# RetNet attention and a gated MLP in one kernel: loads of v behind k, scaling of v on Pool, a third value bank, four more steps transposed by TensorE

## The chip, the cores and the metric

The kernel runs on one core of a Trainium2 chip. A time is the device time of one execution, in microseconds. The compute engines are TensorE (PE, with its weight loads as PEld), VectorE (DVE), ScalarE (ACT) and GpSimd (POOL); SyncE (SP) only issues DMAs here. Each engine takes its instructions in order, and engines wait for each other and for DMAs through semaphores.

## The reference

Eight batches, eight heads, 576 positions, 64 columns a head. The retention has no softmax, only a decay by distance; its result goes through two matrix products with a gelu (sigmoid form) between them.

```python
scores = scale * np.matmul(q, k.transpose(0, 1, 3, 2))
gamma = 1.0 - 2.0 ** (-5.0 - np.arange(H))
rel = pos[:, None] - pos[None, :]
Dmat = np.where(rel >= 0, gamma[:, None, None] ** rel[None, :, :], 0.0)
attn_out = np.matmul(scores * Dmat, v)
x = attn_out.transpose(0, 2, 1, 3).reshape(B * S, H * D)     # 4608 x 512
h = x @ w_in                                                  # 512 x 2048
out = (h * (1.0 / (1.0 + np.exp(-1.702 * h)))) @ w_out        # 2048 x 512
```

## The kernel before, in words

A batch is cut into five chunks of 128 positions (the last has 64), so there are 40 steps; step n is batch n // 5, chunk n % 5. The decay is separated: v is multiplied by a growing factor by key position (`scale_v`, L255, one multiplication of 128 x 512 on VectorE), the result by a falling one by query position (`evac_o`, L356). Inside a chunk the scores are masked to the lower triangle (`mask_s`); what earlier chunks contribute goes through a running state Z = sum of k times v, kept in PSUM (`psZ`) and copied to bf16 by ScalarE in two halves (`evac_z`, L348).

A step is: bring q and k in transposed form into a buffer `qk` (four buffers), `scores` (L281), `mask_s`, `values` (L302: scores times v, the state's update, and the earlier state times q), then `evac_o`, which writes the transposed activations `xT`, and `evac_z`. The transposed form comes in one of two ways. `turn` or a `burst` below step `PE_TURNS` has TensorE transpose (`transposes`, L265, eight matmuls with the identity into `psT`) and ScalarE copy the result out (`evac_t`, L277). From step `PE_TURNS` on, `dma_turn` (L365) has SP issue two DMA transposes, three steps ahead.

The second part works on 512 tokens at a time, nine times. `hidden` (L407) does four matmuls and a gelu on ScalarE for each of 16 column groups, through two PSUM banks in turn; `project` (L425) does the second product, VectorE copies the result out and SP issues its store.

The order is written by hand: each call records instructions for the engines' queues, and waits come from the recorded reads and writes. The prologue (L442 to L505) does steps 0 to 3 and needs all four before the first `hidden`. There, `fill` (L455) gives TensorE matmuls on zeros. Then the 16 `hidden` groups of the first 512 tokens carry step 4 (`turn(4)`), the first 16 `project` groups carry steps 5 to 8 and their transposes, and the 16 `hidden` groups of the next 512 tokens (L537) carry `intra(9)` and `burst(10)` to `burst(13)`. After that a regular pattern of `project`, `hidden` and bursts follows (`region`, L548).

All inputs are fp32 in HBM. Pool issues the loads that cast to bf16 (queue q0, software descriptors): q and k of chunks 0 to 3 of batch 0, `load_w_in(0)`, chunk 4 (`load(0, 4)`: q, k and v), the other three pieces of w_in, four pieces of w_out, then batches 1 and 2. SP loads v of chunks 0 to 3 of batch 0 as fp32 (`load_v32`, L188; queue q1), at the very start; `scale_v` reads these and writes bf16. Before `load(0, 4)` VectorE clears the lower half of chunk 4 (`constants_third`).

The result of the values product lies in a PSUM bank until `evac_o` has read it; in the prologue steps 0 to 3 take two banks in turn (`half`: `psO` and `psU`).

Of the kernel before, what the change touches and what calls it, by code (L numbers as in the profile page):

```python
# [7 lines left out]
ALU = mybir.AluOpType  # L8
# [4 lines left out]
H = 8  # L13
# [5 lines left out]
HP = 4  # L19
# [4 lines left out]
NF = FF // 128  # L24
NST = 3
NQK = 4
PE_TURNS = 10
QK_SCALE = 1.0 / math.sqrt(DH)

IN_ORDER = ("PE", "ACT", "DVE", "POOL", "SP")  # L30
# [92 lines left out]
def bass_retnet_parallel__then__act_gelu_quick_kernel(  # L123
# [9 lines left out]
    R = Rec()  # L133
    es = ExitStack()
    with es:
# [21 lines left out]
        v32 = sb("v32", [P, 4, H * DH], FP32)  # L157
# [20 lines left out]
        def load(b, c):  # L178
            sl, rows = b % NST, ROWS[c]
            for nm, src, dst in (("q", q, st_q), ("k", k, st_k), ("v", v, st_v)):  # L180
                if nm == "v" and b == 0 and c < 4:
                    continue
                s = src[b, :, 128 * c : 128 * c + rows, :].rearrange("h p d -> p h d")
                d = dst[0:rows, sl, c, :].rearrange("p (h d) -> p h d", d=DH)
                R.op("POOL", lambda e, d=d, s=s: e.dma_start(d, s),  # L185
                     w=[(nm, sl, c)], dma=(nm, sl, c))

        def load_v32(c):  # L188
            s = v[0, :, 128 * c : 128 * c + 128, :].rearrange("h p d -> p h d")
            d = v32[:, c, :].rearrange("p (h d) -> p h d", d=DH)  # L190
            R.op("SP", lambda e: e.dma_start(d, s), w=[("v32", c)], dma=("v32", c))

        def load_w_in(i):
            s = moe_w_in.rearrange("(a p) n -> p a n", p=128)[:, :, 512 * i : 512 * i + 512]
            R.op("POOL", lambda e: e.dma_start(w_in_sb[:, :, 512 * i : 512 * i + 512], s),
                 w=[("w_in", i)], dma=("w_in", i))
# [43 lines left out]
        def constants_third(a, b):  # L240
            for t, nm in ((st_q, "q"), (st_k, "k"), (st_v, "v")):
                R.op("DVE", lambda e, t=t: e.memset(t[64:128, a:b, 4, :], 0.0),
                     w=[(nm, sl, 4) for sl in range(a, b)])
# [8 lines left out]
                 r=[("lng", 0, 0), ("lng", 0, 1)], w=["tiny"])  # L252


        def scale_v(n):  # L255
            b, c = divmod(n, NC)
            sl = b % NST
            t = st_v[:, sl, c, :].rearrange("p (h d) -> p h d", d=DH)
            f = vfac[:, :, c : c + 1].to_broadcast([P, H, DH])
            first = b == 0 and c < 4  # L260
            i = v32[:, c, :].rearrange("p (h d) -> p h d", d=DH) if first else t
            R.op("DVE", lambda e: e.tensor_tensor(t, i, f, ALU.mult),  # L262
                 r=["vfac"] + ([("v32", c)] if first else []), w=[("v", sl, c)])

        def transposes(n):  # L265
            b, c = divmod(n, NC)
            sl = b % NST

            def fn(e):
                for a, t in ((0, st_q), (1, st_k)):  # L270
                    for hp in range(HP):
                        i = e.matmul(psT[:, a, hp, :], t[:, sl, c, 128 * hp : 128 * hp + 128],  # L272
                                     ident.ap(), is_transpose=True)
                return i
            R.op("PE", fn, r=["ident", ("q", sl, c), ("k", sl, c)], ps=["T"])
# [26 lines left out]
        def values(n, o=None, z_last=False):  # L302
            po, key = o or (psO, "O")
            b, c = divmod(n, NC)
            sl, N = b % NST, ROWS[c]

            def av(e):
                for hp in range(HP):
                    for hh in range(2):
                        h = 2 * hp + hh  # L310
                        i = e.matmul(po[64 * hh : 64 * hh + 64, hp, 0:N],  # L311
                                     st_v[:, sl, c, 64 * h : 64 * h + 64],
                                     sm[n % 2][:, hh, hp, 0:N],
                                     start=(hp == 0), stop=(c == 0), skip_group_check=True)
                return i
            R.op("PE", av, r=[("sm", n % 2), ("v", sl, c)], ps=[key])
            def add_state():
                if c < 4:
                    def state(e):
                        for hp in range(HP):  # L320
                            for hh in range(2):
                                h = 2 * hp + hh
                                hs = slice(64 * h, 64 * h + 64)
                                i = e.matmul(psZ[64 * hh : 64 * hh + 64, hp, 0:64],  # L324
                                             st_k[:, sl, c, hs], st_v[:, sl, c, hs],
                                             start=(c == 0 and hp == 0), stop=(c == 3),
                                             skip_group_check=True)
                        return i
                    R.op("PE", state, r=[("k", sl, c), ("v", sl, c)], ps=["Z"])

            def add_inter():
                if c > 0:
                    def inter(e):
                        for hp in range(HP):
                            i = e.matmul(po[:, hp, 0:N], zs[(c - 1) % 2][:, hp, :],  # L335
                                         qk[n % NQK][:, 0, hp, 0:N],
                                         start=False, stop=True, skip_group_check=True)
                        return i
                    R.op("PE", inter, r=[("zs", (c - 1) % 2, 0), ("zs", (c - 1) % 2, 1), ("qk", n % NQK, 0)], ps=[key])

            if z_last:
                add_inter()
                add_state()
            else:
                add_state()
                add_inter()

        def evac_z(n):  # L348
            c = n % NC
            for hh in range(2):  # L350
                rows = slice(64 * hh, 64 * hh + 64)
                R.op("ACT", lambda e, rows=rows: e.activation(  # L352
                    zs[c % 2][rows, :, rows], psZ[rows, :, 0:64], AF.Copy),
                    w=[("zs", c % 2, hh)], ps=["Z"])

        def evac_o(n, o=None):  # L356
            po, key = o or (psO, "O")
            b, c = divmod(n, NC)
            N = ROWS[c]
            t0 = S * b + 128 * c  # L360
            R.op("DVE", lambda e: e.tensor_tensor(  # L361
                xT[:, :, t0 : t0 + N], po[:, :, 0:N], gq[:, c, :, 0:N], ALU.mult),
                r=[("gq", min(c, 1))], w=[("xT", b, c)], ps=[key])
# [9 lines left out]
        def turn(n):  # L373
            transposes(n)
            evac_t(n)
            scale_v(n)

        def intra(n):
            scores(n)
            mask_s(n)  # L380
# [58 lines left out]
                     r=[("osb", m)], dma=("osb", m))  # L439


        for c in range(4):  # L442
            load_v32(c)
        constants_first()
        for c in range(4):
            load(0, c)
        load_w_in(0)
        constants_third(0, 1)
        load(0, 4)
        for i in range(1, 4):  # L450
            load_w_in(i)
        for i in range(4):
            load_w_out(i)
# [1 line left out]
        def fill(count):  # L455
            def fn(e):
                for _ in range(count):
                    i = e.matmul(psH[0].ap(), idle[:, 0:128], idle.ap(), start=True, stop=True)  # L458
                return i
            R.op("PE", fn, r=["idle"], ps=[("H", 0)])  # L460

        half = [(psO, "O"), (psU.ap().rearrange("p (h n) -> p h n", h=HP), "U")]
        fill(16)
        transposes(0)
        later_gq(0)
        evac_t(0)
        scale_v(0)
        constants_second()
        scale_v(1)
        later_gq(1)  # L470
        fill(4)
        intra(0)
        transposes(1)
        evac_t(1)
        scale_v(2)
        fill(3)
        intra(1)
        values(0, half[0])
        evac_z(0)
        transposes(2)  # L480
        evac_t(2)
        evac_o(0, half[0])
        later_gq(2)
        later_gq(3)
        scale_v(3)
        fill(3)
        intra(2)
        transposes(3)
        evac_t(3)
        values(1, half[1])  # L490
        evac_z(1)
        evac_o(1, half[1])
        intra(3)
        values(2, half[0])
        evac_z(2)
        evac_o(2, half[0])
        gelu_table()
        fill(3)
        values(3, half[1], z_last=True)
        evac_o(3, half[1])  # L500
        evac_z(3)
        constants_third(1, NST)
        for b in (1, 2):
# [19 lines left out]

        def values_8():
            values(8)
            dma_turn(12)
            finish(8)
            scale_v(10)

        between = {1: lambda: turn(5), 3: burst_5, 6: lambda: burst(6), 9: lambda: burst(7),  # L530
                   12: lambda: burst(8), 14: values_8}
        for i in range(16):
            r, g = divmod(i, 4)
            project(0, r, g, *wide[r % 3])
            if i in between:
                between[i]()
        between = {0: lambda: intra(9), 3: lambda: burst(10), 6: lambda: burst(11),  # L537
                   9: lambda: burst(12), 12: lambda: burst(13)}
        for f in range(NF):
            hidden(1, f)  # L540
# [91 lines left out]
```

## Time and profile before

| | |
|---|---|
| median of three runs | 316.35 us (316.22 to 316.98) |
| the profiled execution | 318.7 us, its span 316.9 us |
| mean granted clock of TensorE | 0.995 |
| busy in the span: PE, ACT, DVE, POOL | 305.2, 128.1, 121.8, 103.8 us |
| first `hidden` matmul | 22.18 us |
| transposes of step 5, of step 6 | 39.08 and 41.82 us |
| software queue q0, hardware queue q1 | 17.83 MB and 17.97 MB |

The span is from the first to the last instruction; the profiled execution's own time has what lies around it. A time in the profile counts from the span's start. A busy TensorE is a pipelined one, so its share says that it had something in flight. The DMA share can be above 1.00, as packets of one engine overlap.

### The profile page before, as it was taken

To read this page: it belongs to the slowest core of one execution; us is meant where nothing else is said; L and a number is where in the kernel's file an instruction comes from. 1 tells how busy PE (TensorE), PEld (TensorE's weight loads), DVE (VectorE), ACT (ScalarE), POOL (GpSimd) and SP (SyncE) were. 2 spreads that over 40 slices of the span, in tenths; PEclk is the share of its full clock that TensorE was granted. 3 is DMA by queue.
4 is the path that set the end of the run, shared out by engine and by line. 5 is a ranking of instruction groups with operands and counts; after the bars stand their busy time and mean duration, and the time that the engine had idled before them with its cause. 6 is when DMAs were issued, how large, how long until landed. Compare 5 with 4: busy or idle time off the path is not lost.

```text
span 316.9 us, 5362 instructions
## 1 busy us (share of the span) xinstructions
PE 305.2 (96%) x2285; PEld 147.1 (46%) x2285; DVE 121.8 (38%) x180; ACT 128.1 (40%) x237; POOL 103.8 (33%) x131
## 2 busy tenths in 40 slices
PE   7679999997999999999999999999999999999995
PEld 2344455443445444444445444444444444444442
DVE  6482067573334533433335334334343341010011
ACT  6487543563334433333334333333334333333300
POOL 9996399465585858332500000000000000000000
PEclk9999999997999999999999999999999999999999
DMA  9999999999999999999992223303330000001111
GB/s 146 173 198 206 180 166 171 156 165 155 136 168 168 166 170 175 168 173 156 148 133 60 67 68 83 78 33 87 81 91 35 34 35 33 35 33 49 50 66 69
DMA packets 153048, 36.14 MB, mean 114 GB/s; under 512 B 144320, under 2 KB 148416, under 8 KB 153024
## 3 DMA queue, kind: packets, MB, share of 16 engines
q0 software_dynamic: 112576, 17.83, 81.9%
q1 hardware_dynamic: 40448, 17.97, 27.2%
q8 instruction: 18, 0.29, 0.4%
q14 instruction: 6, 0.05, 0.0%
HBM read 36.70 MB, written 9.44 MB: 146 GB/s over the span
## 4 chain that ended last, share of the span: by engine, by line
PE 91%; DMA 5%; ACT 2%; POOL 1%; DVE 0%; issue 0%; SPq 0%; POOLq 0%; ACTq 0%
PE psH L414 38%; PE psU L428 34%; PE psH L428 4%; PE psO L311 4%; PE psS L290 4%; PE psO L335 3%; DMA st_k<-in_k_dram 2%; DMA qk<-st_k 2%; PE psZ L324 1%; PE psT L272 1%; PE psO L428 1%; ACT qk L278 1%; POOL st_q L185 1%; ACT gq L246 0%; POOL st_k L185 0%
## 5 line engine op out<-in xcount | busy, mean ns | idle before, releaser
L419 ACT ACTIVATE gT<-psH 128x512 bf16<-128x512 f32 x144 | 86.0, 597 | 139.0 <-PE psH L414 139.0
L414 PE MATMUL psH<-xT,w_in_sb 128*128 128x512 bf16 x576 | 140.8, 381 | 0.5 <-DVE xT L361 0.5
L428 PE MATMUL psU<-w_out_sb,gT 128*128 128x512 bf16 x496 | 121.8, 379 | 0.0
L299 DVE TENSOR_TENSOR sm<-psS,mask 128x1024 bf16<-128x1024 f32 (+1 forms) x40 | 44.7, 1117 | 107.9 <-PE psS L290 107.9
L414 PEld LDWEIGHTS psH<-xT,w_in_sb 128*128 128x128 bf16 x576 | 54.5, 98 | 66.6 <-ACT gT L419 4.1
L428 PEld LDWEIGHTS psU<-w_out_sb,gT 128*128 128x128 bf16 x496 | 47.5, 98 | 53.6
L185 POOL DMA_DIRECT2D st_k<-in_k_dram x40 | 35.0, 875 | 36.2 <-PE psO L335 17.0
L436 DVE COPY osb<-psU 128x512 f32<-128x512 f32 x31 | 21.4, 691 | 56.1 <-PE psU L428 55.4
L185 POOL DMA_DIRECT2D st_q<-in_q_dram x40 | 35.2, 880 | 8.7 <-issue 8.2
L185 POOL DMA_DIRECT2D st_v<-in_v_dram x36 | 31.4, 871 | 12.4 <-issue 8.3
L352 ACT ACTIVATE zs<-psZ 64x256 bf16<-64x256 f32 x64 | 24.2, 378 | 16.3 <-PE psZ L324 15.4
L262 DVE TENSOR_TENSOR st_v<-st_v,vfac 128x512 bf16<-128x512 bf16 x36 | 24.6, 682 | 8.0 <-DMA st_v<-in_v_dram 8.0
L361 DVE TENSOR_TENSOR xT<-psO,gq 128x512 bf16<-128x512 f32 (+1 forms) x38 | 23.8, 627 | 9.5 <-PE psO L335 8.8
L290 PE MATMUL psS<-qk 64*128 64x128 bf16 (+1 forms) x320 | 15.1, 213 | 4.3 <-ACT qk L278 2.2
L290 PEld LDWEIGHTS psS<-qk 64*128 64x128 bf16 x320 | 8.7, 94 | 21.2 <-issue 19.8
L278 ACT ACTIVATE qk<-psT 128x1024 bf16<-128x1024 bf16 x10 | 10.2, 1021 | 16.0 <-PE psT L272 15.9
L311 PE MATMUL psO<-sm,st_v 128*64 128x128 bf16 (+1 forms) x304 | 15.2, 222 | 0.0
L428 PE MATMUL psH<-w_out_sb,gT 128*128 128x512 bf16 x64 | 14.5, 379 | 0.0
L311 PEld LDWEIGHTS psO<-sm,st_v 128*64 128x64 bf16 x304 | 9.4, 110 | 4.7 <-issue 1.4
L335 PE MATMUL psO<-qk,zs 128*128 128x128 bf16 (+1 forms) x120 | 11.3, 217 | 0.0
L458 PE MATMUL psH<-idle 128*128 128x512 bf16 x29 | 9.8, 490 | 1.2 <-DVE idle L212 1.2
L324 PE MATMUL psZ<-st_v,st_k 128*64 128x64 bf16 x256 | 9.5, 197 | 0.0
(43 smaller groups left out, 74.3 us busy)
## 6 DMA issues: line engine op xcount, KB each, us to landing
out_dram<-osb SPq DMA_DIRECT2D x36, 256.0 KB, 2.3
st_q<-in_q_dram POOLq DMA_DIRECT2D x32, 128.0 KB, 20.2
st_k<-in_k_dram POOLq DMA_DIRECT2D x32, 128.0 KB, 20.3
st_v<-in_v_dram POOLq DMA_DIRECT2D x28, 128.0 KB, 20.2
w_in_sb<-in_moe_w_in_dram POOLq DMA_DIRECT2D x4, 512.0 KB, 11.7
w_out_sb<-in_moe_w_out_dram POOLq DMA_DIRECT2D x4, 512.0 KB, 18.8
v<-in_v_dram SPq DMA_DIRECT2D x4, 256.0 KB, 5.1
st_q<-in_q_dram POOLq DMA_DIRECT2D x8, 64.0 KB, 19.6
```

The costliest lines, as they stand in the source:

```text
L185: R.op("POOL", lambda e, d=d, s=s: e.dma_start(d, s), w=[(nm, sl, c)], dma=(nm, sl, c))
L262: R.op("DVE", lambda e: e.tensor_tensor(t, i, f, ALU.mult), r=["vfac"] + ([("v32", c)] if first else []), w=[("v", sl, c)])
L290: i = e.matmul(psS[:, hh, hp, 0:N], t[rows, 1, hp, :], t[rows, 0, hp, 0:N])
L299: R.op("DVE", lambda e: e.tensor_tensor(o, i, m, ALU.mult), r=["mask"], w=[("sm", n % 2)], ps=["S"])
L311: i = e.matmul(po[64 * hh : 64 * hh + 64, hp, 0:N], st_v[:, sl, c, 64 * h : 64 * h + 64], sm[n % 2][:, hh, hp, 0:N], start=(hp == 0), stop ...
L335: i = e.matmul(po[:, hp, 0:N], zs[(c - 1) % 2][:, hp, :], qk[n % NQK][:, 0, hp, 0:N], start=False, stop=True, skip_group_check=True)
L352: R.op("ACT", lambda e, rows=rows: e.activation(zs[c % 2][rows, :, rows], psZ[rows, :, 0:64], AF.Copy), w=[("zs", c % 2, hh)], ps=["Z"])
L361: R.op("DVE", lambda e: e.tensor_tensor(xT[:, :, t0 : t0 + N], po[:, :, 0:N], gq[:, c, :, 0:N], ALU.mult), r=[("gq", min(c, 1))], w=[("xT" ...
L414: i = e.matmul(psH[t].ap(), w_in_sb[:, a, 128 * f : 128 * f + 128], xT[:, a, 512 * c : 512 * c + 512], start=(a == 0), stop=(a == 3))
L419: R.op("ACT", lambda e: e.activation(gT[c % 2][:, f, :], psH[t].ap(), AF.Gelu_apprx_sigmoid), w=[("gT", c % 2, f)], ps=[("H", t)])
L428: i = e.matmul(bank, gT[c % 2][:, f, 128 * r : 128 * r + 128], w_out_sb[:, f, :], start=(f == 0), stop=(f == NF - 1))
L436: R.op("DVE", lambda e: e.tensor_copy(osb[m].ap(), bank), w=[("osb", m)], ps=[key])
```

## The change

Four things change, with the order around them.

SP's fp32 load of v for chunk c carries a read of k of chunk c, so SP waits for k's landing before it issues the load. In the recorded order `load_v32(c)` now follows `load(0, c)`.

`scale_v` takes an engine; chunks 1 to 3 of batch 0 are scaled by Pool. On Pool's queue the scaling of chunk 1 stands behind `load_w_in(0)`, that of chunk 2 behind `load_w_in(1)`, that of chunk 3 behind `load(0, 4)`; the other w_in, w_out and later loads follow. Chunk 0 stays on VectorE, now behind `mask_s(0)`.

The prologue has a third value bank (`psH[1]`) for step 3; steps 0 and 2 use `psO`, step 1 `psU`. `transposes(2)` goes ahead of `values(0)`, the fills are 14, 4, 3, 2, 2, 2 matmuls instead of 16, 4, 3, 3, 3, `later_gq(2)` and `later_gq(3)` and the gelu's table load move.

`PE_TURNS` goes from 10 to 14: steps 10 to 13 are transposed by TensorE and copied out by ScalarE, and their eight DMA transposes on SP go. `turn(10)` goes behind `intra(9)`; `dma_turn(12)` and `scale_v(10)` leave `values_8`.

```diff
-PE_TURNS = 10
+PE_TURNS = 14
@@ load_v32
-            R.op("SP", lambda e: e.dma_start(d, s), w=[("v32", c)], dma=("v32", c))
+            R.op("SP", lambda e: e.dma_start(d, s), r=[("k", 0, c)], w=[("v32", c)], dma=("v32", c))
@@ scale_v
-        def scale_v(n):
+        def scale_v(n, eng="DVE"):
...
-            R.op("DVE", lambda e: e.tensor_tensor(t, i, f, ALU.mult),
+            R.op(eng, lambda e: e.tensor_tensor(t, i, f, ALU.mult),
@@ loads
-        for c in range(4):
-            load_v32(c)
         constants_first()
         for c in range(4):
             load(0, c)
+            load_v32(c)
         load_w_in(0)
+        scale_v(1, "POOL")
+        load_w_in(1)
+        scale_v(2, "POOL")
         constants_third(0, 1)
         load(0, 4)
-        for i in range(1, 4):
+        scale_v(3, "POOL")
+        for i in range(2, 4):
             load_w_in(i)
@@ prologue
-        half = [(psO, "O"), (psU.ap().rearrange("p (h n) -> p h n", h=HP), "U")]
-        fill(16)
+        third = [(psO, "O"), (quarters(psU), "U"), (quarters(psH[1]), ("H", 1))]
+        fill(14)
         transposes(0)
         later_gq(0)
         evac_t(0)
-        scale_v(0)
         constants_second()
-        scale_v(1)
         later_gq(1)
         fill(4)
         intra(0)
+        scale_v(0)
         transposes(1)
         evac_t(1)
-        scale_v(2)
+        later_gq(2)
         fill(3)
         intra(1)
-        values(0, half[0])
-        evac_z(0)
         transposes(2)
         evac_t(2)
-        evac_o(0, half[0])
-        later_gq(2)
-        later_gq(3)
-        scale_v(3)
-        fill(3)
+        values(0, third[0])
+        evac_z(0)
+        evac_o(0, third[0])
+        fill(2)
         intra(2)
         transposes(3)
         evac_t(3)
-        values(1, half[1])
+        later_gq(3)
+        values(1, third[1])
         evac_z(1)
-        evac_o(1, half[1])
+        evac_o(1, third[1])
+        fill(2)
         intra(3)
-        values(2, half[0])
+        values(2, third[0])
         evac_z(2)
-        evac_o(2, half[0])
         gelu_table()
-        fill(3)
-        values(3, half[1], z_last=True)
-        evac_o(3, half[1])
+        evac_o(2, third[0])
+        fill(2)
+        values(3, third[2], z_last=True)
+        evac_o(3, third[2])
         evac_z(3)
@@ after step 8
         def values_8():
             values(8)
-            dma_turn(12)
             finish(8)
-            scale_v(10)
+
+        def intra_9():
+            intra(9)
+            turn(10)
...
-        between = {0: lambda: intra(9), 3: lambda: burst(10), 6: lambda: burst(11),
+        between = {0: intra_9, 3: lambda: burst(10), 6: lambda: burst(11),
```

More of the change, by code (lines that the diff above doesn't have):

```diff
@@ L460, in fill, with quarters @@
             R.op("PE", fn, r=["idle"], ps=[("H", 0)])
-        half = [(psO, "O"), (psU.ap().rearrange("p (h n) -> p h n", h=HP), "U")]
-        fill(16)
+        def quarters(bank):
+            return bank.ap().rearrange("p (h n) -> p h n", h=HP)
+        third = [(psO, "O"), (quarters(psU), "U"), (quarters(psH[1]), ("H", 1))]
+        fill(14)
         transposes(0)
```

## The prediction

> **What bounds the kernel now.** I read the shares of the chain that ended last, then the same chain up to 90 us in order of time, then the waits, the stretches of 5 us, the landing times of single loads, and the timeline where ScalarE shares a stage with the transposes.
>
> Shares of the chain, over the whole span:
>
> ```profile
> PE 91%; DMA 5%; ACT 2%; POOL 1%; DVE 0%; issue 0%; SPq 0%; POOLq 0%; ACTq 0%
> ```
>
> TensorE sets the end; what isn't TensorE lies in the first 75 us. The chain up to 90 us (start, us, what):
>
> ```profile
> 4.17 7.56 DMA st_k<-in_k_dram
> ...
> 22.18 1.90 PE psH L414 x8
> ...
> 37.51 1.73 PE psU L428 x8
> 39.24 0.45 PE psT L272 x8
> 39.69 1.73 PE psU L428 x8
> 41.41 0.33 PE psS L290 x8
> 41.74 0.08 issue
> 41.82 0.61 PE psT L272 x8
> ...
> 67.46 7.13 DMA qk<-st_k
> 74.59 0.14 issue
> 74.72 0.47 PE psS L290 x8
> 75.19 0.57 PE psO L311 x8
> 75.76 0.21 PE psZ L324 x8
> 75.98 0.54 PE psO L335 x4
> 76.52 3.55 PE psH L414 x12
> 80.07 0.86 PE psU L428 x4
> ```
>
> Two places matter: the transposes of step 5 and step 6 at 39.24 and 41.82, which seem free, and the scores of step 13 at 74.72, which wait for a DMA transpose issued at 67.46. Waits up to 130 us (line, for what: us, times, longest), then the two 5 us stretches around the wait (busy us of PE, PEld, DVE, ACT, POOL, clock, DMA share, GB/s):
>
> ```profile
> PE psS L290 <- DMA qk<-st_k: 2.2, 1, 2.2
> ```
>
> ```profile
> 70.00:75.00 5.00, 2.83 (x20) 1.15 (x18) 1.63 (x3) 2.23 (x5) 3.45 (x5) 0.99 1.92 156
> 75.00:80.00 5.00, 5.00 (x38) 2.65 (x34) 2.51 (x3) 1.95 (x4) 3.01 (x4) 0.67 1.78 157
> ```
>
> TensorE stands still for 2.2 us and then runs at a granted clock of 0.67. The landing of the one load of k that step 5 needs (issued at 17.28), by its tile:
>
> ```profile
> DMA to landing us min/median/max: 21.6/21.6/21.6
> ```
>
> It lands at 38.9; its transposes start at 39.1. k of step 6, issued at 19.89, takes 21.8 and lands at 41.7; its transposes start at 41.8. So the DMA queue, not TensorE, is within 0.2 us of setting the pace at 39 to 42: whatever shortens TensorE's prologue is lost there, and whatever delays the queue of loads shows in full.
>
> **Part 1, the last four DMA transposes become TensorE's (steps 10 to 13).** Between 58.1 and 80.1 TensorE's pieces at full clock are 16 groups of hidden at 0.86 (13.8), scores, values and states of the five bursts 0.22, 0.79, 0.79, 1.12, 1.12: 17.9 of 22.0 us. The rest is the 2.2 us wait, 1.6 of half clock after it (0.47 for 0.33, 0.57 for 0.34, 0.21 for 0.12, 0.54 for 0.33, 3.55 for 2.59), 0.3 in scraps. Removed: 3.8. Added: four times eight transposes at 0.45 (row 39.24): 1.8. The loads of k for steps 11 to 13 must then be in by about 62, 65 and 69; step 13's lands at 45.60 + 21.2 = 66.8 now, beside six DMA transposes which go, so I cost it at nothing; its cover is the empty queue.
>
> ScalarE gets four evacuations of 1.02 more. Beside step 9 and in the burst of 10 no evacuation of Z stands with them; there the copy for step 4, at 24.62, is the pattern: the twelve hidden matmuls behind it took 2.68 (chain, at 24.53) for 2.59, so 0.1 each. In the bursts of 11 and 12 the order is evacuation of T, two of Z, then gelu. Timeline of the burst of 11 now:
>
> ```profile
> 66.19 0.77 ACT L352 ACTIVATE zs<-psZ 64x256 bf16<-64x256 f32 x2 [0.21 <-PE psZ L324]
> 67.15 0.60 ACT L419 ACTIVATE gT<-psH 128x512 bf16<-128x512 f32 x1 [0.20 <-PE psH L414]
> ```
>
> The gelu ends at 67.75 and TensorE needs that bank at 67.88. With 1.02 ahead: 0.1 + 1.02 + 0.77 + 0.60 + 0.05 = 2.5 against two groups of hidden, 1.7: 0.75 late. Twice: 1.5. Bounds of this stall: 0 (the next group's order absorbs it) and 1.7. Part 1: -3.8 + 1.8 + 1.5 = -0.5 (ends -2.0 and 0).
>
> **Part 2, the fp32 loads of v wait for k.** Now four loads of 256 KB have queue q1 to themselves until 4.0 (1,823 packets), then share: in 6 to 8 us, q0 moves 1,104 packets and q1 967, where q0 alone moves 1,226 in one us (10 to 11). In the changed kernel q0 starts at 4.0 alone, with the issue pace of Pool (0.87 a load) about equal to 1,024/1,226 = 0.84 us a load. First k at about 4.0 + 1.7 + 0.9 of landing = 6.7 (8.9 now), second at 8.4 (11.7 now). But all 4,096 packets of v now come beside q0 instead of some half of them: at 480 a us a v load lasts 2.1 us, in which q0 loses 2.1 x (1,226 - 550) = 1,400 packets or 1.2 us: 4.6 for four. Now the same sum shows as 15.1 (landing of the last k, 7.63 + 7.5) less 4.0 + 6.9 + 0.9: 3.3. So 1.3 us later for what follows in q0, before any wait; ends 0 (v beside weights costs less) and 2.
>
> SP's queue holds nothing else in that time (its next issue is at 42.17). Behind the waiting loads stand the scalings. An SP load takes 3.4 to 7.1 us to land (these four), 6.1 beside a full queue (the two outputs at 42 and 48). v of chunk 1: 8.4 + 4.2 = 12.6; of chunk 2, k at about 11.5, + 4.5 = 16; of chunk 3, k at about 14.5, + 4.5 = 19, with ends 3.4 and 7.1.
>
> **Part 3, three scalings on Pool, in front of its DMA issues.** Behind the first stand w_in 1; behind the second load(0, 4); behind the third w_in 2 and 3, w_out and all loads of batches 1 and 2. No row shows Pool at elementwise work on 512 columns: DVE takes 0.68 for it; Pool's iota makes 128 columns in 0.23, 0.92 for 512 with no input to read. Lower end 0.7, upper 1.8, taken 1.2, by the iota, the nearest row. [...]
>
> Pool then: 8 loads and w_in 0 issued by 9.3 as now; scaling 1 at 12.6 to 13.8; w_in 1 to 14.7; scaling 2 at 16.0 to 17.2; load(0, 4), three at 0.70, to 19.3; scaling 3 to 20.5; w_in 2 issued by 21.4. From the end of an issue to the first packet is 1.6 (q0's first: 2.43 to 4.0), so w_in 2 starts to move at 23.0, 2.5 to move (0.5 MB at 206 GB/s), 0.9 to land: 26.4. Now it lands at 12.02 + 12.3 = 24.3. Everything behind it is 2.1 us late: k of step 5 at 41.0, of step 6 at 43.8. Ends: 0.2 (v of chunk 2 in at 14.4, Pool at 0.8) and 5 (v of chunks 2 and 3 with 7.1 beside the weights).
>
> **Part 4, three banks, fewer fills, order of the prologue.** values(3) is bound by scaling 3: 20.6, where it starts at 20.66 now; so the first hidden group stays near 22.2 (ends 19.5 and 25), and transposes of step 5 could start at 39.1. Two idle matmuls fewer (27 for 29, 0.22 to 0.43 each), within waits. Worth nothing either way, since the queue sets 41.0: TensorE waits 1.9 us there, then 0.1 at step 6: 43.8 for 41.8. A drop of the clock as at 75 would add up to 1.6; taken as 0.
>
> **Sum.** Queue +2.0, part 1 -0.5: +1.5. The profiled execution took 318.7 (span 316.9, 1.8 around it) and would take 320.2; it stands 2.3 over the median of 316.35, and the change goes on the median: 317.8.
>
> **The rivals.**
>
> *The queue isn't starved: faster.* If v of chunk 2 lands by about 14.5 and Pool scales in 0.8, w_in 2 moves on time and the queue is at most 0.5 late. For it: k is in 2 to 3 us earlier than now, Pool needs only one packet ahead of the queue, w_in 0 and 1 are 5 us of work. Against it: 4.5 us to land is already less than the 6.1 seen beside a full queue. It decides where w_in 2 lands: before about 25, the gain of part 1 is larger. Then +0.3 - 0.5 to -2.0: 314.7 to 316.1, middle 315.2.
>
> *The loads of v are starved beside the weights.* While w_in moves, 408 packets go in 2 us; if queues alternate packet by packet, a v load of 1,024 packets needs as many of the weights', 5 us, not 2. v of chunks 2 and 3 then land at about 19 and 21, scaling 3 ends at 24, w_in 2 lands near 29.3: +5.0 - 0.5 = 320.9. [...]
>
> *The two cancel.* The queue about 0.5 to 1.5 late: within 0.3% of now, about 316.4.
>
> **Chances and range.** Differences of 0.3% (0.95 us) or less can't be told from none. Forecast 0.42 (317.3 to 319.2), starved v 0.16, cancelling 0.17, faster 0.25. That gives slower 0.58, same 0.17, faster 0.25. The range leaves a tenth at each end: 314.6 to 321.0; the forecast's own is 317.3 to 319.2.
>
> **What would show it.** In the changed kernel: w_in 2 lands after 25.5; a wait of TensorE at the transposes of step 5, released by the DMA of st_k, at 40 to 42; Pool idle before its scalings, released by the landing of v; no wait at the scores of step 13, clock 1.00 in 75 to 80; waits of 0.7 at hidden groups in the bursts of 11 and 12, released by gelu. It is wrong if step 5's transposes start before 39.5, or if the bursts show no wait behind ScalarE.

## The result, and the profile after

The kernel after takes 324.65 us (median of four runs, 323.68 to 326.89), the kernel before beside it 316.44 us (316.22 to 316.98): a ratio of 1.027, with a 95% interval of 1.021 to 1.032. That is slower, as forecast, but by 8.2 us and not by 1.5, and above the upper end of the range (321.0). Executions of the kernel before vary: of 29 on one chip, 20 took 316.5 to 317.4 us (granted clock 0.998 or more) and the nine with a lower granted clock (0.989 to 0.995) 317.5 to 321.9, of which the ratio there leaves out the longest. The profiled execution of after took 324.11 us, its span is 322.3 us.

Shares of the chain that ended last, in the kernel after:

```profile
PE 84%; DMA 9%; POOL 4%; issue 1%; ACT 0%; DVE 0%; POOLq 0%
```

TensorE falls from 91% to 84%; DMA and Pool rise from 6% to 13%. In order of time (start, us, what), with the pieces left out marked:

```profile
...
5.92 5.11 DMA st_k<-in_k_dram
11.04 7.28 DMA v<-in_v_dram
18.39 1.05 POOL st_v L262
...
21.51 1.08 POOL st_v L262
22.59 1.49 POOL w_in_sb L195 x2
24.08 2.97 POOL w_out_sb L200 x4
27.05 0.82 POOL st_q L185
27.87 16.75 DMA st_k<-in_k_dram
44.75 0.61 PE psT L272 x8
...
47.54 0.61 PE psT L272 x8
...
75.16 0.59 ACT gT L419
...
80.14 0.59 ACT gT L419
```

After Pool's first issues the chain goes through k of chunk 2 to the load of v that waits for it, to the scaling on Pool that waits for that, to the load of k for step 5, which Pool now issues at 27.87 (17.28 before) and which lands at 44.61 (38.92 before). The transposes of step 5 stand at 44.75 (39.24 before), those of step 6 at 47.54 (41.82): 5.5 and 5.7 us later, and nothing of it is won back.

Three of the waits up to 130 us, those on which the reading rests (line, for what: us in all, times, longest):

```profile
POOL st_v L262 <- DMA v<-in_v_dram: 7.2, 2, 6.9
PE psT L272 <- DMA st_k<-in_k_dram: 2.0, 1, 2.0
PE psH L414 <- ACT gT L419: 1.3, 2, 0.7
```

The 2.0 us are only the last part of the delay at step 5. TensorE was ready for these transposes at 42.75, itself 3.5 us later than before, since its prologue is late too: it waits 1.1, 1.4 and 0.4 us for scaled v, its clock is 0.50 from 14 to 26 us, and the first `hidden` starts at 24.70 for 22.18. The late v thus reaches step 5 by two ways, the load queue and the prologue, and the queue is the later one.

Pool's own timeline around the scalings (start, us, what, in brackets the idle time before and its releaser):

```profile
8.52 0.83 POOL L195 DMA_DIRECT2D w_in_sb<-in_moe_w_in_dram  x1
16.23 1.06 POOL L262 TENSOR_TENSOR st_v<-v,vfac 128x512 bf16<-128x512 f32 x1 [6.89 <-DMA v<-in_v_dram]
17.24 0.81 POOL L195 DMA_DIRECT2D w_in_sb<-in_moe_w_in_dram  x1
18.39 1.05 POOL L262 TENSOR_TENSOR st_v<-v,vfac 128x512 bf16<-128x512 f32 x1 [0.35 <-DMA v<-in_v_dram]
...
21.50 1.09 POOL L262 TENSOR_TENSOR st_v<-v,vfac 128x512 bf16<-128x512 f32 x1
22.50 1.58 POOL L195 DMA_DIRECT2D w_in_sb<-in_moe_w_in_dram  x2
```

Pool waits for 6.9 us, and from 9.35 to 17.24 it issues no load. What that does to the transfers is in the 5 us stretches of before (busy us of PE, PEld, DVE, ACT, POOL, then clock, DMA share, GB/s):

```profile
0.00:5.00 5.00, 3.81 (x9) 1.34 (x10) 3.55 (x19) 3.97 (x12) 4.32 (x11) 1.00 0.75 123
5.00:10.00 5.00, 3.53 (x19) 1.57 (x18) 1.98 (x5) 1.46 (x4) 5.00 (x8) 1.00 1.87 184
10.00:15.00 5.00, 3.42 (x55) 2.11 (x53) 2.71 (x3) 2.63 (x4) 5.00 (x9) 1.00 2.32 163
15.00:20.00 5.00, 3.62 (x70) 2.50 (x68) 4.14 (x6) 4.52 (x9) 5.00 (x8) 1.00 1.54 192
20.00:25.00 5.00, 4.46 (x44) 2.33 (x42) 3.96 (x7) 4.26 (x9) 5.00 (x7) 1.00 1.24 207
```

and of after, with two single us in which the software queue moved only 12 and 32 packets:

```profile
0.00:5.00 5.00, 3.81 (x9) 1.34 (x10) 3.54 (x19) 3.96 (x12) 4.31 (x11) 1.00 0.53 34
5.00:10.00 5.00, 4.68 (x37) 2.23 (x35) 1.62 (x4) 3.03 (x6) 4.35 (x6) 1.00 2.07 151
10.00:15.00 5.00, 3.04 (x44) 1.72 (x44) 2.79 (x4) 3.11 (x5) 0.00 (x0) 0.82 1.64 199
15.00:20.00 5.00, 3.64 (x40) 2.34 (x38) 1.92 (x2) 2.39 (x4) 3.42 (x4) 0.50 0.96 164
20.00:25.00 5.00, 3.92 (x46) 2.46 (x44) 2.81 (x4) 2.92 (x6) 5.00 (x8) 0.50 1.29 131
...
18.00:19.00 1.00, 1.00 (x14) 0.62 (x10) 0.16 (x1) 0.75 (x2) 0.65 (x2) 0.50 0.52 37
24.00:25.00 1.00, 0.57 (x9) 0.26 (x8) 0.84 (x2) 0.68 (x2) 1.00 (x3) 0.50 0.73 33
...
75.00:80.00 5.00, 4.30 (x48) 2.33 (x48) 2.42 (x3) 3.36 (x7) 3.88 (x5) 1.00 2.24 158
```

The last column accounts for most of the delay of the loads. Both kernels load the same inputs. Added up (5 us times GB/s), before has moved 1,535 KB by 10 us and 4,345 KB by 25; after has moved 925 and 3,395. The missing 950 KB are 4.6 us at the 206 GB/s at which the weights go (25 to 30 us in before), of the 5.7 us by which k of step 5 is late. 610 KB of it, 3.0 us, are missing already at 10 us: before moves v in the first microseconds, when the software queue has nothing to move yet, and after leaves that time empty (34 GB/s for 123). In 10 to 15, 180 KB are made up. The other 520 KB, 2.5 us, go in 15 to 25, where Pool's late issues let the queue run dry.

The last row answers the stretch that the prediction showed at a clock of 0.67: in after it runs at 1.00. The burst of step 13 itself now stands at 80 to 85 us; the clock is 1.00 there too, and no scores of step 13 wait.

The whole difference sits ahead of 86 us. Here it is cut into three, with a second profile of the kernel before (below), whose time is the ordinary one: the start of the second 512 tokens' first `hidden`, the length of that stretch of 16 groups with its bursts, and the rest of the span.

| us | starts | lasts | rest of the span | span |
|---|---|---|---|---|
| before, profile shown first | 58.08 | 21.99 | 236.8 | 316.9 |
| before, second profile | 58.02 | 19.89 | 236.8 | 314.7 |
| after | 63.80 | 21.73 | 236.8 | 322.3 |

Against the second profile: +5.8 ahead of the stretch (parts 2 to 4), +1.8 in it (part 1), nothing behind it; 7.6 together, which is the difference of the spans.

### The profile page after: what moved, and what is told of

Its sections match the earlier page's. It is cut to its first block, busy times and chain, and to the rows that moved or that the text cites. A ratio compares the mean times of both kernels' runs of the same rounds, so it can differ in the third digit from the quotient of the medians.

```text
span 322.3 us, 5373 instructions
## 1 busy us (share of the span) xinstructions
PE 307.4 (95%) x2273; PEld 149.9 (46%) x2315; DVE 120.0 (37%) x177; ACT 131.7 (41%) x241; POOL 107.2 (33%) x134
## 4 chain that ended last, share of the span: by engine, by line
PE 84%; DMA 9%; POOL 4%; issue 1%; ACT 0%; DVE 0%; POOLq 0%
PE psH L414 34%; PE psU L428 32%; DMA st_k<-in_k_dram 7%; PE psH L428 4%; PE psO L311 4%; PE psS L290 3%; PE psO L335 3%; DMA v<-in_v_dram 2%; PE psT L272 1%; POOL st_q L185 1%; PE psZ L324 1%; PE psO L428 1%; POOL w_out_sb L200 1%; POOL st_k L185 1%; POOL st_v L262 1%
## 5 line engine op out<-in xcount | busy, mean ns | idle before, releaser
L414 PE MATMUL psH<-xT,w_in_sb 128*128 128x512 bf16 x559 | 138.6, 381 | 2.9 <-ACT gT L419 1.3
L428 PE MATMUL psU<-w_out_sb,gT 128*128 128x512 bf16 x476 | 118.6, 379 | 1.1
L299 DVE TENSOR_TENSOR sm<-psS,mask 128x1024 bf16<-128x1024 f32 (+1 forms) x40 | 44.7, 1117 | 107.1 <-PE psS L290 107.1
L278 ACT ACTIVATE qk<-psT 128x1024 bf16<-128x1024 bf16 x14 | 14.3, 1024 | 20.1 <-PE psT L272 20.1
## 6 DMA issues: line engine op xcount, KB each, us to landing
st_q<-in_q_dram POOLq DMA_DIRECT2D x32, 128.0 KB, 16.3
```

What stands on the lines that cost most here:

```text
L299: R.op("DVE", lambda e: e.tensor_tensor(o, i, m, ALU.mult), r=["mask"], w=[("sm", n % 2)], ps=["S"])
L414: i = e.matmul(psH[t].ap(), w_in_sb[:, a, 128 * f : 128 * f + 128], xT[:, a, 512 * c : 512 * c + 512], start=(a == 0), stop=(a == 3))
L428: i = e.matmul(bank, gT[c % 2][:, f, 128 * r : 128 * r + 128], w_out_sb[:, f, :], start=(f == 0), stop=(f == NF - 1))
```

## The experiments

Every run's profile ends with the same 236.8 us, so each is read by the two columns above. Each run stands beside runs of the kernel before on the same chip. Since these vary, a difference of two medians and the ratio of the same two kernels need not agree.

### The four parts taken apart

Part 1 alone, on the kernel before:

```diff
-PE_TURNS = 10
+PE_TURNS = 14
@@ after step 8
-            dma_turn(12)
             finish(8)
-            scale_v(10)
+        def intra_9():
+            intra(9)
+            turn(10)
-        between = {0: lambda: intra(9), ...
+        between = {0: intra_9, ...
```

> The kernel before with part 1 alone (steps 10 to 13 transposed by TensorE). If part 1 is worth what the profiled execution of before shows, -0.5 as predicted: about 316.0 and no wait at the scores of step 13. If the ordinary run of before loses less at step 13 than its profiled execution (318.7 against a median of 316.4), the gain of 3.8 is only about 1.5 there and the transposes and the waits behind ScalarE cost 3.3: about 318.2.

Measured: 318.85 us (318.28 to 319.77, 12 runs) beside 316.93 (316.28 to 320.0); ratio 1.003 (1.001 to 1.006). The stretch lasts 21.73 us, the same as in after, with the same two waits for gelu of 0.65 us and none at step 13. Part 1 is a loss: 0.3% by the ratio, 1.8 us by the stretch against an ordinary execution of before.

Parts 2 to 4 alone, on the kernel after:

```diff
-PE_TURNS = 14
+PE_TURNS = 10
@@ after step 8: as in the kernel before
+            dma_turn(12)
+            scale_v(10)
-        between = {0: intra_9, ...
+        between = {0: lambda: intra(9), ...
```

> The changed kernel with PE_TURNS back at 10, so parts 2 to 4 alone. Theory (Pool waits for v in front of its own DMA issues, the load queue runs dry): transposes of step 5 start at 44 to 45, time 5.5 to 6 over before: 322. If part 1 has a share of its own in the 8 us, this run stays 1.5 to 2.5 below the changed kernel. Rival (all of it is the prologue): as the changed kernel, 324.6.

Measured: 323.11 us (322.24 to 324.56, 6 runs); ratio 1.018 (1.015 to 1.021). v lands at 12.5, 17.7, 18.8 and 20.8, w_in 2 at 29.53, k of step 5 at 45.41; the stretch starts at 64.6 and lasts 20.1. The parts add up: without part 1 the stretch lasts 1.6 us less than in after, and the rest of the loss is here. By the ratios the two give 2.1% together, at the low end of the interval of the whole change.

The scalings back on VectorE, the wait of SP kept:

```diff
-        scale_v(1, "POOL")
         load_w_in(1)
-        scale_v(2, "POOL")
...
-        scale_v(3, "POOL")
@@ prologue, each behind an evac_o or evac_z
+        scale_v(1)
+        scale_v(2)
+        scale_v(3)
```

> The changed kernel with the scalings of chunks 1 to 3 on VectorE; SP's loads of v still wait for k. Theory (Pool's wait starves the queue): k of step 5 lands within 1.5 us of before (38.9 to 40.4), transposes of step 5 at 39 to 40.5, about 318.5 to 319.5. Rival (it is the packets of v beside the loads, wherever the scaling stands): k of step 5 still lands after 43, time about 324.

Measured: 325.33 us (323.18 to 325.88, 4 runs); ratio 1.023 (1.019 to 1.027). The theory that Pool's standing alone makes the loss fell here. Pool issues as before (w_in 1 at 9.24, batch 1 from 16.41), nothing is gained, and k of step 5 lands at 43.69, as the rival had it. The chain of this run (start, us, what) and its waits of VectorE for v:

```profile
7.63 6.51 DMA st_k<-in_k_dram
...
14.16 10.87 DMA v<-in_v_dram
...
25.05 0.70 DVE st_v L262
...
27.77 3.59 PE psH L414 x8
...
46.62 0.45 PE psT L272 x8
```

```profile
DVE st_v L262 <- DMA v<-in_v_dram: 7.5, 4, 2.8
```

The load of v of chunk 3 now takes 10.9 us to land, that of chunk 2 11.1 (6.9 and 7.3 in after), since the weights that Pool no longer holds back move beside them (313 packets of the software queue beside 311 of q1 from 16 to 18 us, where after has 42 beside 1,720). The first `hidden` starts at 27.77, three us later than in after, and step 5 at 46.62 waits for TensorE's own late prologue: k of step 5 was in at 43.69.

The wait undone, Pool's scalings kept:

```diff
-            R.op("SP", ..., r=[("k", 0, c)], w=[("v32", c)], dma=("v32", c))
+            R.op("SP", ..., w=[("v32", c)], dma=("v32", c))
@@ loads
+        for c in range(4):
+            load_v32(c)
         constants_first()
         for c in range(4):
             load(0, c)
-            load_v32(c)
```

> The changed kernel with the loads of v issued at the start, without a wait for k; the scalings stay on Pool. Theory (it is the wait for v, not Pool's work): Pool's scalings cost three times 1.06 us of issue time and the queue, 20 us deep at landing, doesn't run dry; k of step 5 lands at 39 to 40, about 318.5. Rival (scaling on Pool by itself holds up the queue): k of step 5 lands after 41.5.

Measured: 318.98 us (318.16 to 319.61, 10 runs); ratio 1.004 (1.002 to 1.007), the same as part 1 alone. v is in at 3.9 to 10.4, Pool issues w_in 2 at 15.20, w_in 2 lands at 24.37 (24.28 before), k of step 5 at 39.65. By 25 us 4,365 KB have moved, as before. The first 5 us, and the chain's first `hidden` and transposes of step 5:

```profile
0.00:5.00 5.00, 3.81 (x9) 1.34 (x10) 3.55 (x19) 3.97 (x12) 4.32 (x11) 1.00 0.74 123
```

```profile
23.52 1.90 PE psH L414 x8
...
40.58 0.45 PE psT L272 x8
```

Both stand 1.3 us later than in the kernel before, in an execution whose clock was at 0.53 from 10 to 15 us. So three scalings on Pool, the third bank and the new order cost at most some tenths beside part 1 alone (318.98 for 318.85); the wait for k is what costs.

### The kernel before once more, and how many steps TensorE should take

Since part 1 lost where the sum had a gain, the kernel before was profiled a second time, unchanged.

> The kernel before once more, for a second profile. If the first profile (318.7, 2.3 over its median) is dear because of step 13, this one, if its time is near 316.5, has the stretch from the first hidden group of the second 512 tokens to the end of the last at 20 to 20.5 us instead of 22.0, with a shorter wait and no drop of the clock. If step 13 is the same here, the 2.3 lie elsewhere, and part 1 removes 3.8 in every run.

Measured: 316.52 us, span 314.7. Its chain at step 13, and its one wait there:

```profile
67.03 6.96 DMA qk<-st_k
...
74.12 0.40 PE psS L290 x8
...
75.32 2.16 PE psH L414 x10
```

```profile
PE psS L290 <- DMA qk<-st_k: 1.6, 1, 1.6
```

TensorE waits 1.6 us here, not 2.2, and goes on at full clock: scores in 0.40 for 0.47, ten `hidden` matmuls in 2.16, where twelve took 3.55. The first profile was dear in this one place by 2.1 us of 2.2 that separate the spans.

`PE_TURNS` 11 and 12, each with `turn(10)` behind `intra(9)` and the DMA transposes of the other steps kept:

```diff
-PE_TURNS = 10
+PE_TURNS = 11
@@ after step 8
-            scale_v(10)
+        def intra_9():
+            intra(9)
+            turn(10)
```

> The kernel before with PE_TURNS at 11: only step 10 goes to TensorE, two DMA transposes fewer ahead of step 13's. If step 13's load of q is late because of the six transposes before it (66.2 instead of about 62), two fewer bring its transposes some 2.5 us earlier: the wait of 2.2 and the drop of the clock are gone for 0.45 to 0.55 on TensorE and no evacuation of Z beside it. Then 0.5 to 1.5 below an ordinary run of before, 315.3 to 316.3. If the wait was already small in ordinary runs: +0.5, 317.3.

Measured: 315.86 us (315.61 to 316.64, 12 runs) beside 317.17 (316.53 to 321.86, 29 runs); ratio 0.9955 (0.9936 to 0.9975). It beats both kernels, the one before by 0.4%. One wait of TensorE is left in the stretch, at the scores of step 11:

```profile
PE psS L290 <- DMA qk<-st_k: 1.1, 1, 1.1
```

The stretch lasts 20.1 us there, no less than the ordinary 19.9 of before. But this profiled execution was the slowest of the twelve, and the others took 315.6 to 316.1; that they have no such wait is only likely, as in the next run. All twelve lie closer together than those of the kernel before.

> The kernel before with PE_TURNS at 12: steps 10 and 11 by TensorE, both without an evacuation of Z behind the copy. About 0.5 over the kernel with 11. If the cost of part 1 lies in the bursts of 11 and 12, where the copy stands ahead of two evacuations of Z (0.7 each at the next hidden group), this run is 1.4 + 0.9 below the one with 14 (318.9): 316.5.

Measured: 316.08 us (315.78 to 316.58, 10 runs); ratio 0.9964 (0.9947 to 0.9981). No wait of TensorE above 0.1 us is left in the stretch, which lasts 19.2. With 14, transposes and gelu waits are added and there is no more wait to remove.

Part 1 alone, with the copies of Z ahead of the transposes' copy on ScalarE:

```diff
             values(n - 1)
+            zfirst = 10 < n < PE_TURNS and (n - 1) % NC < 4
+            if zfirst:
+                evac_z(n - 1)
             if n + 1 < PE_TURNS:
```

> Part 1 alone (PE_TURNS 14), with the evacuations of Z put ahead of the copy of the transposes on ScalarE in the bursts of 11 and 12. The work on ScalarE is the same, but it starts 0.55 earlier, at the state's matmuls: the waits of 0.7 behind gelu go down to about 0.15 each, 1.1 below part 1 alone: 317.8. If these waits are not on the path: 318.9.

Measured: 317.33 us (317.05 to 317.96, 10 runs); ratio 1.000 (0.998 to 1.002). The stretch lasts 20.4 us for 21.7 of part 1 alone: 1.3 less, as much as the two gelu waits of part 1.

### The wait alone

On the kernel before, only the loads of v changed:

```diff
-            R.op("SP", ..., w=[("v32", c)], dma=("v32", c))
+            R.op("SP", ..., r=[("k", 0, c)], w=[("v32", c)], dma=("v32", c))
@@ loads
-        for c in range(4):
-            load_v32(c)
         constants_first()
         for c in range(4):
             load(0, c)
+            load_v32(c)
```

> The kernel before with one edit: each load of v waits for k of its chunk. Theory now (the wait makes v late, and late v loads must share with the weights that Pool has already queued): v of chunk 3 lands at 24 to 26, first hidden group at 26 to 28 instead of 22.2, k of step 5 at about 43; time 5 to 8 over before, 322 to 325, with VectorE waiting for v and no wait on Pool. If the loss needed Pool's scaling (the predicted mechanism alone): within 1 us of before, 317.5.

Measured: 327.03 us (325.53 to 327.69, 4 runs) beside 318.31 (315.72 to 321.32, 7 runs); ratio 1.030 (1.022 to 1.037). The wait alone loses as much as the whole change. Its chain and wait:

```profile
14.22 12.16 DMA v<-in_v_dram
...
32.98 1.90 PE psH L414 x8
...
50.03 0.45 PE psT L272 x8
```

```profile
DVE st_v L262 <- DMA v<-in_v_dram: 15.7, 4, 7.0
```

v of chunk 3 takes 12.2 us to land. In the order of before, VectorE has the scalings ahead of the masks of the scores, so every wait for v stops TensorE's prologue too (it waits 12.2 us for masks), and `hidden` starts at 32.98. The stretch starts at 68.74 but lasts only 18.20: by then no DMA transpose is late, and 1.7 of the loss comes back.

All four loads of v behind k of chunk 0 only:

```diff
-            R.op("SP", ..., w=[("v32", c)], dma=("v32", c))
+            R.op("SP", ..., r=[("k", 0, 0)], w=[("v32", c)], dma=("v32", c))
@@ loads: load_v32(c) behind load(0, c)
```

> The kernel before with half the wait: all four loads of v wait for k of chunk 0 only, so SP issues them in a row at about 7. Theory now: they go beside the casting loads of q and k, packet for packet as in before, and are done before the weights get thick: v of chunk 3 lands at 14 to 17, transposes of step 5 at 39.5 to 41, 0 to 2 over before. If any wait for k is ruinous: as the run with four waits, 322 or more.

Measured: 322.01 us (321.33 to 322.28, 4 runs); ratio 1.013 (1.007 to 1.018). v of chunk 3 was expected by 17 at the latest and lands at 22.75, that of chunk 2 takes 12.2 us. The loads were not issued in a row either: the issues of chunks 2 and 3 took SP 3.0 and 2.4 us, where 0.37 is usual with the waits, and the last one started at 10.8. `hidden` starts at 29.46, the stretch at 65.22 and lasts 18.19. The stretch starts 7.2 us late, where the full wait makes it 10.7: with the loads of v issued up to 3.4 us earlier a third of that is undone, by the ratios more than half. The later v moves, the more it costs.

The runs side by side (us):

| | stretch starts | lasts | first `hidden` | v of chunk 3 lands | k of step 5 lands |
|---|---|---|---|---|---|
| before, second profile | 58.02 | 19.89 | 22.25 | 10.0 (first profile) | 38.9 (first profile) |
| part 1 alone | 59.45 | 21.73 | 23.68 | | |
| no wait, scalings on Pool | 59.29 | 21.73 | 23.52 | 10.37 | 39.65 |
| after | 63.80 | 21.73 | 24.70 | 20.55 | 44.61 |
| parts 2 to 4 | 64.6 | 20.1 | 25.85 | 20.80 | 45.41 |
| wait, scalings on VectorE | 65.34 | 21.73 | 27.77 | 25.03 | 43.69 |
| wait alone | 68.74 | 18.20 | 32.98 | 26.38 | 42.41 |
| wait for the first k | 65.22 | 18.19 | 29.46 | 22.75 | 43.53 |

The profile of part 1 alone starts its stretch 1.4 us late although its prologue is that of before; the variant with Z first, with the same prologue, starts it at 58.08. That is one execution's prologue, whose clock stood at 0.67 from 10 to 15 us, and no part of part 1.

## Why the prediction was right or wrong

**Right: the direction, the path and the place.** Each step of part 3 is in the trace: Pool idle before a scaling and released by v, w_in 2 landing after 25.5 (28.32), TensorE waiting 2.0 us at step 5's transposes for the DMA of `st_k` (1.9 forecast), then next to nothing at step 6. Only the time is another, 42.7 to 44.7 instead of 39.1 to 41.0. Part 4 was taken as nothing, and the run without the wait agrees, to some tenths. Its first `hidden` "near 22.2" came at 24.70, and the drop of the clock "taken as 0" came too (0.50 from 14 to 26 us). Neither shows in the time, because k of step 5 was later still: that the prologue hid behind the queue was forecast, that it would be 3.5 us late was not.

**Wrong: "v of chunk 1: 8.4 + 4.2 = 12.6; of chunk 2 16; of chunk 3 19".** This is the step that failed in part 3. The landings of k were right: SP issued the loads of v at 6.9, 8.7, 11.0 and 13.7, for 6.7, 8.4, 11.5 and 14.5 forecast. The time for an SP load to land was too short: 5.2, 7.5, 7.3 and 6.9 us were measured, for 4.2 to 4.5, chosen from the lower half of the text's own rows (3.4 to 7.1, and 6.1 beside a full queue). v of chunk 1 landed at 16.16. It stood behind v of chunk 0 on the same queue, whose first packet moved 1.9 us after its issue, and beside the loads of q and k: from 8 to 12 us the software queue moved 3,281 packets and q1 1,069. The upper end that the text had itself, 7.1, was nearly the truth for three of the four. The scalings then stood at 16.2, 18.4 and 21.5 for 12.6, 16.0 and 19.3.

**Mis-sized: "everything behind it is 2.1 us late".** k of step 5 is 5.7 late. w_in 2 lands 4.0 late, after Pool's later issue; 1.7 more appear between w_in 2 and k (16.3 us for 14.6). Some 0.8 of these are bytes missing from 25 to 35 us, where the transfers run at 195 and 187 GB/s for 206 and 207. What slows them there, no run shows.

**Mis-sized: contention, "+1.3 us".** By the bytes, leaving the first microseconds unused is 3.0 us by itself at 10 us, and 2.1 still at 15. The step asked what v costs beside q and k; the larger cost is that the time in which v moved for nothing stays empty. In the sum this term was covered by Pool's lateness, so it could be off without showing; with Pool on time (the run with the scalings on VectorE) it is what remains, k of step 5 4.8 late. Some 2.8 of these are accounted for by bytes missing at 30 us, the rest is not.

**Wrong: part 1 as a gain, -0.5.** "Removed: 3.8" was the cost of the wait in one execution that stood 2.3 us over the median, and the forecast was put on the median. In an ordinary execution the wait is 1.6 and the clock stays, and a sum against the median can't remove what the median doesn't have. The added terms were right: four groups of transposes at 0.45 to 0.55 are 2.0 (1.8 forecast), two gelu waits 1.3 (1.5). With them -1.6 + 2.0 + 1.3 and 0.1 in scraps is +1.8, which is what the stretch shows. The profiled execution's surplus was in plain sight, as a clock of 0.67 in one 5 us stretch.

**The rivals.** The times are those of the starved v, chance 0.16: v of chunks 2 and 3 at 19 and 21 (18.3 and 20.6), scaling 3 done at 24 (22.6), w_in 2 near 29.3 (28.3), +5.0 on the queue (+5.7). With part 1 put right it would have been 323.2. Its mechanism, packets in turn beside the weights, is not what happens in after, since there the weights have mostly stopped: from 16 to 18 us q1 moves 1,720 packets and the software queue 42. That its times came near is therefore in part luck. Once Pool doesn't wait, the counts are those of its mechanism: in the run with the scalings on VectorE the software queue and q1 moved 313 and 311 packets from 16 to 18 us, and 804 and 805 from 20 to 22. From 8 to 12 us in after they are three to one (3,281 and 1,069); what sets the share in either case, no run shows. The unstarved queue and the cancelling are out: the queue ran dry twice.

**The price of a scaling on Pool.** 1.2 was taken, 1.05 to 1.09 measured, and VectorE takes 0.69 for the same operands: a factor of 1.5. It hardly matters: without the wait, three of them cost nothing that shows.

What stays open: what slows the loads at 25 to 35 us in after, what else than missing bytes delays k with the scalings on VectorE, and how much of the loss is Pool's standing in a kernel where v lands late anyway. The runs show only that with Pool waiting and with Pool free the kernel comes out nearly alike (324.65 and 325.33 us): what the free queue wins at step 5, 0.9 us, the prologue loses by a v that lands 4.5 us later.

## What to carry to other kernels

A load that is moved behind another costs what it used to get for nothing. Count the bytes that both kernels have moved by the same time, here by 10 and by 25 us, before pricing any wait: the missing bytes over the rate gave 4.6 of the 5.7 us by which the last load needed was late, and 2.8 of 4.8 with the scalings on VectorE. And where an engine both computes and issues loads, a wait ahead of its issues passes to everything behind them (here Pool's 6.9 us idle is on the way to the load of k for step 5, issued at 27.87 for 17.28).

Before a stall is charged to a change, look whether the profiled execution is the median one. A wait that carries a clock drop in one execution (here 2.2 us, then 0.67) and none in the next (1.6 us, then 1.00) is worth the smaller of the two against a median. To transpose one or two more steps on TensorE (`PE_TURNS` 11 or 12 here) shortens the wait or takes it away for less than it costs, 0.4% of the time; four more don't.

## What the runs showed of the hardware

The same four loads of v on the hardware queue landed 3.4 to 7.1 us after their issue at the start of the kernel before, 5.2 to 7.5 in after, 6.1 to 9.0 in parts 2 to 4 alone with the same prologue, and, but for the first of each run, 9.3 to 12.2 in the wait alone and with the scalings on VectorE, where Pool goes on issuing loads (busy for 5.00 of every 5 us from 5 to 25 us, in after for 0.00 from 10 to 15). With the one wait for k of chunk 0, the issue of a load of v held SP for up to 3.0 us.

A wait of 1.6 us at step 13 left the clock at 1.00, one of 2.2 was followed by 0.67 over the next 5 us. In the profile of part 1 alone, a wait of 3.8 us that ended at 10.4 was followed by 0.67 from 10 to 15. In the prologue of after TensorE was busy for 4.7 of the 5 us from 5 to 10, its longest waits from 9 to 14 us were 0.6 and 1.1 us, and the granted clock was 0.50 from 14 to 26 us. So a drop stood behind one wait of 3.8 us, behind one of 2.2 and behind none longer than 1.1, and what brings it about no run shows.
